# Decode attention with a gated unit: the last pair's values in the slot of the last keys but one, gate's weights in the slot of the values

## The chip, the core and the metric

The kernel runs on one core of one Trainium2 chip. The metric is the device time of one execution in microseconds (us); three executions are given, and one more was profiled. All data are 32-bit floats.

## What is computed

One token passes through an attention over a cache of 8192 keys and values for each of 32 heads, and through a gated linear unit; the product of both is added to the input.

```python
# x: 1 x 512, k_cache and v_cache: 32 heads x 8192 x 128, wq: 512 x 4096, wo: 4096 x 512
xn = layernorm(x)
q = (xn @ wq) by heads                       # 32 x 128
p = softmax((q . k_cache) / sqrt(128))       # 32 x 8192
s = (p @ v_cache, heads side by side) @ wo   # 512
h = sigmoid(xn @ w_gate) * (xn @ w_up)       # 1376
g = silu(h @ w_down)                         # 512
out = x + s * g
```

Keys and values are 134 MB each, the weights some 26 MB. Each byte is read once.

## The kernel before

Heads are taken in 16 pairs (`NP = 16`, i from 0 to 15). A pair's keys, and a pair's values, are one load of 8.4 MB: 128 partitions with 128 rows of 128 elements each, the first head in the lower 64 partitions, the second in the upper 64.

There are three buffers of that size, `slots[0]` to `slots[2]`; together they take most of the core's memory. Keys of pair i go to slot `i % 2` and values of every pair to slot 2 (`issue`, L115 to L117). wq is loaded to slot 2 ahead of everything. The weights of the gated unit (`load_gate`, L88) go to slot `NP % 2`, which is slot 0, in three loads (w_gate and w_up at L92, w_down's first 1280 rows at L95), with a fourth for w_down's last 128 rows into a tile of its own (L96). wo (`load_wo`, L102) goes to slot 1 in five loads (L106).

All of these loads are issued by SP, in the order of the list `order`: wq, keys 0, keys 1, values 0, keys 2, values 1, and so on to keys 15, values 14, values 15, gate, wo. `need(item)` issues the list up to and with that item. An issue waits on SP until the slot's last readers are done, and whatever stands behind it on SP waits too. Each transfer counts up one of eight completion counters that are handed out in turn, and waits for that counter's former transfer.

For pair i the loop does this. VectorE multiplies the keys by the query in place (`times_query`, L263) and sums the rows (`row_sums`, L268), in two halves. Between the first multiplication and the first sum of pair i stand the maximum and the exponentials of pair i - 1 (`all_max`, L278 to L285), the two small DMAs of ScalarE that place the heads of pair i - 2 in `o_all` (`place`, L314), and TensorE's work on the values of pair i - 1 (`values`, L295 to L301). At the end of the loop's body come `need("v", i)`, the next keys, and the row maximum (`row_max`, L272 and L274). So the values of pair i are consumed one turn of the loop after its keys.

Pair 14 (`NP - 2`) has no keys two pairs ahead, and `need` is skipped there; pair 15 issues the rest of the list, up to wo.

After the loop: the values of pair 15, the two matrix products of the gated unit (`glu_row`, L201), `place` of pair 15, the unit's hidden layer and output (`glu_hidden`, L208 to L213; `glu_out`, L228 to L233), and the projection by wo in the five parts in which it lands (`project`, L320 and L324, with a fold over partitions at L219 and L221). VectorE multiplies, adds the input, and SP stores.

Of the kernel before, what the change touches and what calls it, by code (L numbers as in the profile page):

```python
# [18 lines left out]
def kernel(  # L19
# [19 lines left out]
    NP = H // 2  # L39
# [24 lines left out]
    slots = [stream.tile([P, SLOT], F32, name=f"slot{i}") for i in range(3)]  # L64
# [12 lines left out]
    def load_rows(which, src, t, i):  # L77
        rows = src.rearrange("b h s d -> (b h s) d")[2 * i * S:2 * (i + 1) * S, :]
        nc.sync.dma_start(t, rows.rearrange("(p j) d -> p (j d)", p=P))
        kv_t[which, i] = t  # L80
# [5 lines left out]
    assert FW + GP <= QT and FL % GP == 0 and 2 * KT * F + FP * D <= SLOT  # L86

    def load_gate():  # L88
        t = slots[NP % 2]
        for n, (name, src) in enumerate((("wg", w_gate), ("wu", w_up))):  # L90
            v = t[:, n * KT * F:(n + 1) * KT * F].rearrange("p (k f) -> p k f", f=F)
            nc.sync.dma_start(v, src.rearrange("(p k) f -> p k f", k=KT))  # L92
            gl[name] = v
        v = t[:, 2 * KT * F:2 * KT * F + FP * D].rearrange("p (c e) -> p c e", e=D)
        nc.sync.dma_start(v, w_down[:FP * P, :].rearrange("(p r) e -> p r e", r=FP))  # L95
        nc.sync.dma_start(wd_last, w_down[F - P:, :])  # L96
        gl["wd"] = [v[:, c, :] for c in range(FP)] + [wd_last]
# [12 lines left out]
    order = [("wq", 0), ("k", 0)]  # L110
# [3 lines left out]

    def issue(which, i):  # L115
        dict(wq=load_wq, gate=load_gate, wo=load_wo, k=lambda: load_rows("k", k_cache, slots[i % 2], i),
             v=lambda: load_rows("v", v_cache, slots[2], i))[which]()  # L117

    ahead = iter(order)
    loaded = set()  # L120
# [1 line left out]
    def need(*item):  # L122
        while item not in loaded:
            nxt = next(ahead)
            issue(*nxt)
            loaded.add(nxt)
# [54 lines left out]
    def spread(t):  # L181

        b, g = divmod(t, NG)
        pb = big(f"pb{t}")
        nc.tensor.matmul(pb, ones[g * GP:g * GP + 1, :], q_row[g * GP:g * GP + 1, b, :],  # L185
                         start=True, stop=True)
        qb[t] = work.tile([P, 2, Dh], F32, tag="qb", name=f"qb{t}", bufs=2)
        for e, h in enumerate(HALF):
            nc.scalar.copy(qb[t][h], pb.rearrange("p (i e d) -> p i e d", e=2, d=Dh)[h, :, e, :])  # L189
# [71 lines left out]
    def times_query(i, j):  # L261
        q = qb[i // 2][:, i % 2:i % 2 + 1, :]
        nc.vector.tensor_mul(key_rows(i, j), key_rows(i, j), q.to_broadcast([P, SB, Dh]))  # L263

    def row_sums(i, j):
        if j == 0:
            sc[i] = work.tile([P, NB], F32, tag="sc", name=f"sc{i}", bufs=2)
        nc.vector.reduce_sum(sc[i][:, j:j + SB], key_rows(i, j), axis=AX.X)  # L268

    def row_max(i):  # L270
        mx[i] = work.tile([P, 4], F32, tag="mx", name=f"mx{i}", bufs=2)
        nc.vector.reduce_max(mx[i][:, 0:1], sc[i], axis=AX.X)  # L272
        pt = ps_s.tile([1, P], F32, tag="ps_s", name=f"pt{i}")
        nc.tensor.matmul(pt, mx[i][:, 0:1], ident, start=True, stop=True)  # L274
        return pt

    def all_max(i, pt):
        nc.vector.reduce_max(mx[i][:1, 1:3], pt.rearrange("o (e p) -> o e p", e=2), axis=AX.X)  # L278
        pm = ps_s.tile([P, 2], F32, tag="ps_s", name=f"pm{i}")
        nc.tensor.matmul(pm, ones[:1, :], mx[i][:1, 1:3], start=True, stop=True)  # L280
        rs[i] = work.tile([P, 1], F32, tag="rs", name=f"rs{i}", bufs=2)
        for e, h in enumerate(HALF):
            nc.scalar.mul(mx[i][h, 3:4], pm[h, e:e + 1], -SCALE)  # L283
        for e, h in enumerate(HALF):
            nc.scalar.activation(weights[h, :, e * HT:(e + 1) * HT],  # L285
                                 sc[i][h].rearrange("p (g b) -> p g b", b=HT), AF.Exp,
                                 bias=mx[i][h, 3:4], scale=SCALE, accum_out=rs[i][h])

    def values(i):
        row = pn[i % 2]  # L290
        nc.tensor.matmul(row[:, Dh:], half, rs[i], start=True, stop=True)  # L291

        for j in range(0, NB, HT):
            g = j // HT % NG
            nc.tensor.matmul(po[i % 2][g * GP:g * GP + 2 * HT, :], weights[:, j // HT, :],  # L295
                             kv_t["v", i][:, j * Dh:(j + HT) * Dh],
                             start=(j < HT * NG), stop=(j >= NB - HT * NG))
        o1 = work.tile([P, QT], F32, tag="o1", name=f"o1_{i}")
        nc.scalar.copy(o1, po[i % 2])  # L299
        for b in range(HT):  # L300
            nc.tensor.matmul(row[:, :Dh], pick[:, b:2 * HT:HT], o1[:, b * Dh:(b + 1) * Dh],  # L301
                             start=(b == 0), stop=(b == HT - 1))

    def heads_out(i):
        rl = work.tile([2, 1], F32, tag="rl", name=f"rl{i}", bufs=2)
        nc.vector.reciprocal(rl, pn[i % 2][:, Dh:])  # L306
        on = work.tile([2, Dh], F32, tag="on", name=f"on{i}", bufs=2)
        nc.vector.tensor_scalar(on, pn[i % 2][:, :Dh], rl, None, op0=ALU.mult)
        return on

    def place(i, on):
        for e in range(2):
            p0 = (2 * i + e) * WP
            nc.scalar.dma_start(o_all[p0:p0 + WP, :], on[e:e + 1, :].rearrange("o (a r) -> o a r", r=WR))  # L314
# [17 lines left out]
    for i in range(NP):  # L332
        if i % 2 == 1 and i + 1 < NP:
            spread(i // 2 + 1)
        times_query(i, 0)
        if i > 0:
            all_max(i - 1, pt)
            if on is not None:
                place(i - 2, on)
            need("v", i - 1)  # L340
            values(i - 1)
        row_sums(i, 0)
        for j in range(SB, NB, SB):
            times_query(i, j)
            row_sums(i, j)

        need("v", i)
        if i != NP - 2:
            need(*(("k", i + 2) if i + 2 < NP else order[-1]))
        pt = row_max(i)  # L350
        if i > 0:
            on = heads_out(i - 1)
# [42 lines left out]
```

## Time and profile before

| | |
|---|---|
| three runs | 702.3, 703.5, 703.5 us (median 703.5) |
| the profiled execution | 702.62 us |
| its span from first to last instruction | 700.8 us |
| DMA traffic | 294.00 MB, mean 420 GB/s |
| VectorE busy | 576.9 us (82%) |
| TensorE busy (matmuls) | 231.3 us (33%) |
| ScalarE busy | 43.4 us (6%) |
| mean granted TensorE clock | 0.659 of full speed |

The page cuts the span into 40 slices of 17.5 us and prints a busy share for each engine, in tenths, so that a stretch in which something stops is seen at a glance. The chain of work that ended last is followed back from the last instruction, each step to what released it; in order of time it tells what the next step waited for. SPq stands for SP's instruction queue, in which the loads are issued. Times in the rows are in us from the start of the span.

### The profile page before, as it was taken

To read this page: it belongs to the slowest core of one execution; us is meant where nothing else is said; L and a number is where in the kernel's file an instruction comes from. 1 tells how busy PE (TensorE), PEld (TensorE's weight loads), DVE (VectorE), ACT (ScalarE), POOL (GpSimd) and SP (SyncE) were. 2 spreads that over 40 slices of the span, in tenths; PEclk is the share of its full clock that TensorE was granted. 3 is DMA by queue.
4 is the path that set the end of the run, shared out by engine and by line. 5 is a ranking of instruction groups with operands and counts; after the bars stand their busy time and mean duration, and the time that the engine had idled before them with its cause. 6 is when DMAs were issued, how large, how long until landed. Compare 5 with 4: busy or idle time off the path is not lost.

```text
span 700.8 us, 3712 instructions
## 1 busy us (share of the span) xinstructions
PE 231.3 (33%) x1570; PEld 61.7 (9%) x1570; DVE 576.9 (82%) x171; ACT 43.4 (6%) x138; POOL 0.7 (0%) x6
## 2 busy tenths in 40 slices
PE   0510150516051422505061504324061505033556
PEld 0100010101010100101010101001010101001121
DVE  0259999999999989898998989898998989796020
ACT  0010010001010000000001000000001000001010
POOL 0000000000000000000000000000000000000000
PEclk9955575757575575757575666657575756657698
DMA  9999999999999999999999999999999999958996
GB/s 415 423 419 419 464 412 438 420 423 426 460 424 426 427 449 431 430 426 446 430 434 426 442 434 434 431 434 434 438 431 430 434 441 431 430 218 352 391 432 272
DMA packets 6481, 294.00 MB, mean 420 GB/s; under 512 B 1080, under 2 KB 1088, under 8 KB 1472
## 3 DMA queue, kind: packets, MB, share of 16 engines
q1 hardware_dynamic: 6056, 293.74, 97.2%
q8 instruction: 12, 0.20, 0.1%
q10 hardware_dynamic: 408, 0.02, 0.0%
q14 instruction: 5, 0.04, 0.0%
HBM read 293.74 MB, written 0.00 MB: 419 GB/s over the span
## 4 chain that ended last, share of the span: by engine, by line
DMA 68%; PE 19%; DVE 11%; issue 0%; ACT 0%; SPq 0%; ACTq 0%; DVEq 0%
DMA slot<-in_A_v_cache_dram 57%; PE po L295 19%; DVE slot L263 6%; DMA slot<-in_A_k_cache_dram 6%; DMA slot<-in_A_wo_dram 5%; DVE sc L268 5%; PE acc L320 1%; PE acc L324 0%; PE pm L280 0%; ACT s_acc L219 0%; DVE mx L272 0%; ACTq L314 0%; ACT weights L285 0%; SPq L106 0%; DVE mx L278 0%
## 5 line engine op out<-in xcount | busy, mean ns | idle before, releaser
L263 DVE TENSOR_TENSOR slot<-slot,qb 128x8192 f32<-128x8192 f32 x32 | 277.8, 8681 | 43.5 <-DMA slot<-in_A_k_cache_dram 43.5
L268 DVE TENSOR_REDUCE sc<-slot 128x64 f32<-128x8192 f32 x32 | 277.7, 8679 | 0.9 <-DVE mx L278 0.3
L295 PE MATMUL po<-slot,weights 128*8 128x512 f32 x1024 | 147.2, 740 | 104.6 <-DMA slot<-in_A_v_cache_dram 104.6
L280 PE MATMUL pm<-mx,ones 1*128 1x2 f32 x32 | 9.3, 358 | 145.9 <-DVE mx L278 145.9
L274 PE MATMUL pt<-ident,mx 128*1 128x128 f32 x32 | 9.3, 392 | 143.4 <-DVE rl L306 103.2
L295 PEld LDWEIGHTS po<-slot,weights 128*8 128x8 f32 x1024 | 28.7, 104 | 209.8 <-DMA slot<-in_A_v_cache_dram 106.1
L299 ACT COPY o<-po 128x512 f32<-128x512 f32 x16 | 9.4, 585 | 256.6 <-PE po L295 256.6
L280 PEld LDWEIGHTS pm<-mx,ones 1*128 1x128 f32 x32 | 7.9, 306 | 161.3 <-DVE mx L278 161.3
L306 DVE RECIPROCAL rl<-pn 2x1 f32<-2x1 f32 x16 | 2.3, 146 | 23.6 <-PE pn L301 23.6
L301 PE MATMUL pn<-o,pick 128*2 128x128 f32 x128 | 16.6, 272 | 11.5 <-ACT o L299 11.5
L283 ACT ACTIVATE mx<-pm 64x1 f32<-64x1 f32 x32 | 5.3, 165 | 225.5 <-PE pm L280 225.1
L147 DVE TENSOR_REDUCE st<-x_col 128x1 f32<-128x4 f32 x1 | 0.2, 156 | 21.9 <-DMA x_col<-in_A_x_dram 21.9
L185 PE MATMUL pb<-q_row,ones 1*128 1x512 f32 x16 | 15.6, 1075 | 0.0
L274 PEld LDWEIGHTS pt<-ident,mx 128*1 128x1 f32 x32 | 1.8, 80 | 148.1 <-issue 148.1
L285 ACT ACTIVATE weights<-sc,mx 64x128 f32<-64x128 f32 x32 | 12.8, 399 | 0.8
L189 ACT COPY qb<-pb 64x256 f32<-64x256 f32 x16 | 5.9, 366 | 108.1 <-PE pb L185 108.0
L301 PEld LDWEIGHTS pn<-o,pick 128*2 128x2 f32 x128 | 9.6, 84 | 28.6 <-ACT o L299 26.3
L364 DVE TENSOR_TENSOR g_row<-g_row,acc 128x128 f32<-128x128 f32 x1 | 0.3, 289 | 14.2 <-PE acc L324 14.2
L291 PE MATMUL pn<-rs,half 128*2 128x1 f32 x32 | 3.0, 164 | 24.9 <-ACT weights L285 24.9
L320 PE MATMUL acc<-slot,o_all 128*1 128x512 f32 x56 | 9.7, 781 | 3.7 <-DMA slot<-in_A_wo_dram 3.7
L174 PE MATMUL pq<-slot,xn 128*1 128x512 f32 x64 | 9.5, 757 | 1.4 <-DVE pq L165 1.4
L143 PE MATMUL p_sum<-st,ones 128*128 128x1 f32 x2 | 0.6, 362 | 23.3 <-DVE st L147 23.3
(65 smaller groups left out, 65.6 us busy)
## 6 DMA issues: line engine op xcount, KB each, us to landing
slot<-in_A_wo_dram SPq DMA_DIRECT2D x1, 3584.0 KB
slot<-in_B_w_gate_dram SPq DMA_DIRECT2D x1, 2752.0 KB
slot<-in_B_w_up_dram SPq DMA_DIRECT2D x1, 2752.0 KB
slot<-in_B_w_down_dram SPq DMA_DIRECT2D x1, 2560.0 KB
slot<-in_A_wo_dram SPq DMA_DIRECT2D x1, 2560.0 KB
slot<-in_A_wo_dram SPq DMA_DIRECT2D x1, 1024.0 KB
slot<-in_A_wo_dram SPq DMA_DIRECT2D x1, 768.0 KB
o_all<-on ACTq DMA_DIRECT2D x32, 0.5 KB
```

The source lines that it names most:

```text
L174: nc.tensor.matmul(pq[b][g * GP:g * GP + 1, :], xn[:, k:k + 1], gl["wq"][:, k, c:c + QT], start=(k == 0), stop=(k == KT - 1))
L185: nc.tensor.matmul(pb, ones[g * GP:g * GP + 1, :], q_row[g * GP:g * GP + 1, b, :], start=True, stop=True)
L189: nc.scalar.copy(qb[t][h], pb.rearrange("p (i e d) -> p i e d", e=2, d=Dh)[h, :, e, :])
L263: nc.vector.tensor_mul(key_rows(i, j), key_rows(i, j), q.to_broadcast([P, SB, Dh]))
L268: nc.vector.reduce_sum(sc[i][:, j:j + SB], key_rows(i, j), axis=AX.X)
L274: nc.tensor.matmul(pt, mx[i][:, 0:1], ident, start=True, stop=True)
L280: nc.tensor.matmul(pm, ones[:1, :], mx[i][:1, 1:3], start=True, stop=True)
L285: nc.scalar.activation(weights[h, :, e * HT:(e + 1) * HT], sc[i][h].rearrange("p (g b) -> p g b", b=HT), AF.Exp, bias=mx[i][h, 3:4], scale ...
L295: nc.tensor.matmul(po[i % 2][g * GP:g * GP + 2 * HT, :], weights[:, j // HT, :], kv_t["v", i][:, j * Dh:(j + HT) * Dh], start=(j < HT * NG ...
L299: nc.scalar.copy(o1, po[i % 2])
L301: nc.tensor.matmul(row[:, :Dh], pick[:, b:2 * HT:HT], o1[:, b * Dh:(b + 1) * Dh], start=(b == 0), stop=(b == HT - 1))
L320: nc.tensor.matmul(acc4[g:g + 1, :], o_all[:, r:r + 1], gl["wo"][:, r, :], start=(r < NG), stop=(r + NG >= W_FOLD))
```

## The change

Values of pair 15 go to slot `NP % 2`, which is slot 0, in place of slot 2. Gate's weights go to slot 2 in place of slot 0. At the end of pair 14's turn, where nothing was issued beyond its own values, the values of pair 15 are issued as well. The list `order` stays as it is, and so does every instruction of the computing engines.

```diff
     def load_gate():
-        t = slots[NP % 2]
+        t = slots[2]
...
-             v=lambda: load_rows("v", v_cache, slots[2], i))[which]()
+             v=lambda: load_rows("v", v_cache, slots[2 if i < NP - 1 else NP % 2], i))[which]()
...
         need("v", i)
-        if i != NP - 2:
-            need(*(("k", i + 2) if i + 2 < NP else order[-1]))
+        if i + 2 < NP:
+            need("k", i + 2)
+        elif i + 2 == NP:
+            need("v", i + 1)
+        else:
+            need(*order[-1])
         pt = row_max(i)
```

## Rows read from the trace of the kernel before

**Rows 1.** The page: busy time of the engines, GB/s by slice, the chain's shares.

```profile
PE 231.3 (33%) x1570; PEld 61.7 (9%) x1570; DVE 576.9 (82%) x171; ACT 43.4 (6%) x138; POOL 0.7 (0%) x6
...
GB/s 415 423 419 419 464 412 438 420 423 426 460 424 426 427 449 431 430 426 446 430 434 426 442 434 434 431 434 434 438 431 430 434 441 431 430 218 352 391 432 272
...
DMA 68%; PE 19%; DVE 11%; issue 0%; ACT 0%; SPq 0%; ACTq 0%; DVEq 0%
```

**Rows 2.** The chain in order of time, last stage: start, duration, what.

```profile
555.98 29.82 DMA slot<-in_A_v_cache_dram
...
585.84 9.89 PE po L295 x64
...
595.75 29.29 DMA slot<-in_A_v_cache_dram
...
625.08 9.05 PE po L295 x64
...
634.14 21.75 DMA slot<-in_A_v_cache_dram
```

**Rows 3.** The timeline, VectorE and TensorE: start, duration, instruction, idle time before it.

```profile
566.60 8.69 DVE L263 TENSOR_TENSOR slot<-slot,qb 128x8192 f32<-128x8192 f32 x1 [3.14 <-DMA slot<-in_A_k_cache_dram]
...
592.71 8.69 DVE L268 TENSOR_REDUCE sc<-slot 128x64 f32<-128x8192 f32 x1
...
605.78 8.69 DVE L263 TENSOR_TENSOR slot<-slot,qb 128x8192 f32<-128x8192 f32 x1 [3.62 <-DMA slot<-in_A_k_cache_dram]
...
631.90 8.69 DVE L268 TENSOR_REDUCE sc<-slot 128x64 f32<-128x8192 f32 x1
...
644.07 0.19 PE L291 MATMUL pn<-rs,half 128*2 128x1 f32 x2 [1.47 <-ACT weights L285]
...
655.93 8.93 PE L295 MATMUL po<-slot,weights 128*8 128x512 f32 x64 [11.68 <-DMA slot<-in_A_v_cache_dram]
```

**Rows 4.** The timeline of SP's queue: start, duration, load issued.

```profile
562.73 0.33 SPq L79 DMA_DIRECT2D slot<-in_A_k_cache_dram  x1
...
634.56 0.38 SPq L92 DMA_DIRECT2D slot<-in_B_w_gate_dram  x1
...
635.47 0.54 SPq L95 DMA_DIRECT2D slot<-in_B_w_down_dram  x1
```

**Rows 5.** SP's own waits, 600 to 640 and 640 to 701: total, times, longest.

```profile
SPq L79 <- DMA slot<-in_A_v_cache_dram: 29.0, 1, 29.0
SPq L79 <- PE po L295: 9.1, 1, 9.1
...
SPq L96 <- DMA slot<-in_A_v_cache_dram: 19.9, 1, 19.9
...
SPq L106 <- DMA o_all<-on: 4.0, 1, 4.0
```

**Rows 6.** Stretches: length, busy time by engine, clock, DMA share, GB/s.

```profile
625.00:634.20 9.20, 8.99 (x64) 1.74 (x64) 9.16 (x2) 0.05 (x1) 0.00 (x0) 0.78 0.01 2
...
655.90:695.30 39.40, 29.10 (x270) 7.44 (x270) 4.12 (x18) 3.19 (x5) 0.00 (x0) 0.82 0.99 421
...
685.50:688.00 2.50, 2.49 (x12) 0.40 (x16) 0.00 (x0) 0.00 (x0) 0.00 (x0) 0.50 0.97 418
...
690.50:692.00 1.50, 1.24 (x12) 0.19 (x10) 0.00 (x0) 0.00 (x0) 0.00 (x0) 1.00 1.00 415
```

**Rows 7.** The timeline of TensorE after the last pair's values, columns as in rows 3.

```profile
669.11 2.57 PE L201 MATMUL pwu<-slot,xn 128*1 128x320 f32 x56 [0.31 <-DMA slot<-in_B_w_up_dram]
...
676.42 4.01 PE L228 MATMUL pd<-slot,hid 128*1 128x512 f32 x18 [4.74 <-DMA slot<-in_B_w_down_dram]
...
685.51 6.05 PE L320 MATMUL acc<-slot,o_all 128*1 128x512 f32 x28 [3.48 <-DMA slot<-in_A_wo_dram]
...
691.82 3.60 PE L320 MATMUL acc<-slot,o_all 128*1 128x512 f32 x28 [0.26 <-DMA slot<-in_A_wo_dram]
```

## The prediction

> **What bounds the kernel now.** I read the profile's page first. VectorE is busy 82% of the span and TensorE 33%, yet the transfers run at 412 GB/s or more in the first 35 slices, and the chain that ended last is 68% DMA [rows 1]. So the kernel is a stream of 294 MB, and what counts is whether that stream ever stops. Slice 35 (613 to 631 us) falls to 218 GB/s and slice 36 to 352: something stops there and nowhere else before the end [rows 1].
>
> Second I read the chain in order of time over the last stage. It is a plain alternation: a load of values lands, 64 matmuls consume it (9.89 and 9.05 us), the next load of values is issued the moment they end, and so on [rows 2]. In the steady loop that costs nothing: while TensorE consumes values, the engines carry the next keys, already queued. The landings show it: keys of pair 14 at 566.6, values 13 at 585.8, keys 15 at 605.7, values 14 at 625.0, one load of 8.4 MB each 19.2 to 19.9 us [rows 2, 3].
>
> Third, SP's queue, its waits and the stretch itself. After keys 15 there are no more keys to cover the next gap. The load of values 15 targets slot 2, which values 14 hold until the matmuls end at 634.13; it is issued at 634.14 [rows 2]. The queue had waited 29.0 us for values 14 to land and then 9.1 us for their matmuls [rows 5]. From 625.0 to 634.2 the engines moved 2 GB/s [rows 6]. The lone load then takes 21.75 us from issue to landing at 655.89 [rows 2].
>
> Fourth, what follows that landing. Gate's three large loads were issued at 634.6 to 635.5 and lie in the queue behind values 15; the stretch from 655.9 to 695.3 runs at 421 GB/s without a stop [rows 4, 6]. TensorE waits there for w_up 0.31 us, w_down 4.74, the first part of wo 3.48 and the second 0.26 [rows 7]. So the end is paced by the stream.
>
> **The change, part by part.** *Values 15 to slot 0.* Slot 0 held keys 14. VectorE's last pass over them starts at 592.71 and lasts 8.69 us, so the slot is free at 601.4 [rows 3]. SP issues values 14 at 595.75 [rows 2], then stands at this wait for 5.7 us; nothing else is in its queue that could go earlier, since gate needs slot 2 and wo needs slot 1, which VectorE reads until 640.6 [rows 3]. At 601.4 keys 15 are still landing (until 605.7) and values 14 are queued, so values 15 become the third load outstanding. Three outstanding were there at 562.73 too, when keys 15 were issued behind keys 14 (landing 566.6) and values 13, and they landed 19.2 and 19.9 us apart [rows 2, 3, 4]. So values 15 should follow values 14 at that distance: landing at 625.04 + 19.2 to 19.9 = 644.3 to 645.0 instead of 655.89. I take 19.4, the middle of the three distances 19.2, 19.9 and 19.3: 644.4. Gain: 30.85 − 19.4 = 11.4 us (bounds 10.9 and 11.6). The same from the parts: 9.10 us of stopped stream plus 21.75 − 19.4 = 2.35 us for a load that starts on an idle queue.
>
> The Trainium skill, "DMA: Bandwidth & Descriptors", section "Anatomy of one DMA", puts the fixed cost of a transfer at about 2.0 us, there for another issuing path; the gain by it would be 9.1 + 2.0 = 11.1 us. The rows give 2.35, and I go by the rows.
>
> *Gate to slot 2.* The four loads now wait for the matmuls on values 14, at 634.13, in place of values 15. They were issued at 634.56 and after [rows 4], so their issue hardly moves. They must be queued before values 15 finish; a load needs 2.35 us to start, so the last useful moment is 644.4 − 2.35 = 642.0. Cover: 7.4 us. Without it, each us of delay past 642.0 is a us of stopped stream. The smaller fourth load, w_down's last rows, writes no slot and still waited 19.9 us for values 15 to land [rows 5]: some issues also wait for an earlier transfer's completion counter. In the changed kernel it may wait so until 644.4, and wo stands behind it in SP's queue; but w_gate, w_up and w_down (8.3 MB, about 19 us) are queued ahead, so that wait is covered by some 17 us. The last part of wo waited 4.0 us for a small o_all transfer [rows 5]; that transfer comes earlier with the rest.
>
> *The removed condition.* Program order of the other engines is untouched; no instruction is added or taken away, so nothing is to be costed on TensorE, VectorE or ScalarE themselves.
>
> *What is late next.* The weights of pair 15 depend on VectorE: its last pass starts at 631.90 and the first matmul of pair 15 runs at 644.07 [rows 3]. Values 15 would arrive at 644.3 or later, so VectorE's chain and the stream meet within a us; if the weights come last they cost nothing yet, because TensorE next waits for w_up (0.31 us) and w_down (4.74 us), which move with the stream [rows 7]. So everything after the landing moves by 11.4 us with the same distances.
>
> *TensorE's clock in the tail.* The same 64 matmuls took 9.89, 9.05 and 8.93 us [rows 2, 3]; the difference is how soon after an idle stretch the granted clock goes from 0.50 (1.2 GHz) to 1.00 (2.4 GHz), as it does between 688 and 690.5 in the last stage [rows 6]. In the last stage the first part of wo took 6.05 us for 28 matmuls and the second 3.60 for as many, at a wait of only 0.26 us between them [rows 7]. If the rise comes 0.9 us less lucky there, the end moves by 0.9 − 0.26 = 0.6 us. A luckier rise gains nothing, for the second part of wo lands when it lands. Bounds 0 and +0.6; I take +0.2, nearer the two equal rows.
>
> *Sum.* Profiled execution: 702.62 (span 700.8 and 1.8 around it) − 11.4 + 0.2 = 691.4. The four known times, 702.3, 702.62, 703.5 and 703.5, have a mean of 703.0, 0.4 above the profiled one; so 691.8. From the bounds: 702.3 − 11.6 = 690.7 to 703.5 − 10.9 + 0.6 = 693.2.
>
> **The rivals.**
> (a) *Gate is held until values 15 land*, by a reused completion counter as the fourth load was [rows 5]. Then the queue runs dry at 644.4 and restarts 2.35 us later: 694.2. Against it: w_gate went 0.42 us after values 15 [rows 4], so it waited for nothing that was in flight then; and the order of transfers on the counters changes little.
> (b) *The tail stays at the lower clock* because the stages have moved against it: the second part of wo 6.05 instead of 3.60, and the closing 1.9 us of matmuls and fold about double: +4 us, 695.8. Against it: the clock rose within the first part of wo, which ran through [rows 6, 7], and that part keeps its length.
> (c) *Values 14 and 15 share the engines* rather than queue. Values 14 then land late, by up to 19.4 us; their matmuls end late, slot 2 comes free late, and gate with all behind it starts late. The stream stops as soon as values 14 land after 642.0 − 9.05 = 632.9, and the gain is gone when they land at 644.4. There it turns slower: with the matmuls at the slowest pace (the lower clock throughout, about 13.5 us by 6.05 for 28) gate goes out at 657.9, starts at 660.2, against 655.9 before: about +4.4 us, 707. The Trainium skill, same page, section "Queues, rings and completion order", says that an engine takes its descriptors in ring order but that a later one may finish first; the first half speaks against this rival, the second for a trace of it. The rows decide: three loads outstanding landed a full 19.2 and 19.9 us apart [rows 2, 3].
> (d) *The change doesn't do what it says*: a wait for values 14's matmuls remains on values 15, say through the order that the framework keeps. Then 703.5. Against it: keys 15 in slot 1 were issued at 562.73 without regard to values 13 in slot 2 [rows 3, 4], so waits go by slot.
>
> **How the numbers follow.** Forecast 691.8: 0.90. (a) 694.2: 0.04. (b) 695.8: 0.02. (c) 707: 0.02. (d) 703.5: 0.02. The forecast's own range 690.7 to 693.2 and a few tenths for the runs' spread give 690.3 to 693.8, which leaves out (a) to (d) and a little more. A measurement can tell about 0.2% (1.4 us) from no change: faster 0.96, same 0.02, slower 0.02.
>
> **What would show it.** Right: values 15 issued near 601.5 and w_gate near 634.2; more than 400 GB/s in slices 35 and 36; values 15 consumed from 644 to 645, with a wait before them of under 1 us where 11.7 us stood [rows 3]; the waits for w_down and wo as before, all 11 to 12 us earlier; the end of the chain leading from wo back through the stream. Wrong: values 14 landing after 626; a stretch under 300 GB/s around 645; a wait for w_gate; the issue of values 15 near 634.

## The result, and the profile after

The changed kernel takes 690.4 us (median of six runs, 690.0 to 691.8) against 703.3 us: a ratio of 0.982, 95% interval 0.981 to 0.983. That is 12.9 us less; the forecast was 691.8. Between the two profiled executions the span went from 700.8 to 688.7 us, 12.1 us less.

The page of the changed kernel first: transfers in GB/s by slice, and the chain's shares by engine, to be read beside [rows 1].

```profile
GB/s 407 446 426 426 426 412 438 427 426 426 426 432 426 438 457 427 434 426 435 430 426 438 449 431 426 427 445 430 426 439 438 434 426 442 443 426 428 417 423 267
...
DVE 56%; DMA 42%; PE 1%; issue 0%; ACT 0%; ACTq 0%; SPq 0%; DVEq 0%
```

The hole of 218 and 352 GB/s is gone; no slice but the last is below 407. The queue of SP in the same stage (start, duration, load issued; compare [rows 2, 4]):

```profile
601.56 0.33 SPq L79 DMA_DIRECT2D slot<-in_A_v_cache_dram  x1
630.02 0.33 SPq L92 DMA_DIRECT2D slot<-in_B_w_gate_dram  x1
632.84 0.33 SPq L92 DMA_DIRECT2D slot<-in_B_w_up_dram  x1
634.59 0.33 SPq L95 DMA_DIRECT2D slot<-in_B_w_down_dram  x1
645.47 0.33 SPq L96 DMA_DIRECT2D wd_last<-in_B_w_down_dram  x1
```

Values 15 are issued at 601.56 where they went out at 634.14. Gate's loads go out one by one from 630.02, each as soon as the matmuls on its own columns of slot 2 are done. Two stretches (length, busy time of PE, PEld, DVE, ACT, POOL, granted clock, DMA share, GB/s; compare [rows 6]):

```profile
625.00:634.20 9.20, 9.20 (x64) 1.74 (x56) 9.16 (x2) 0.00 (x0) 0.00 (x0) 0.71 1.03 443
...
645.50:683.00 37.50, 29.29 (x270) 7.77 (x270) 4.12 (x18) 3.19 (x5) 0.00 (x0) 0.79 0.98 417
```

While TensorE consumes values 14, the engines now move 443 GB/s instead of 2. TensorE's timeline (start, duration, instruction, idle time before it and what ended it; compare [rows 3, 7]):

```profile
643.63 0.19 PE L291 MATMUL pn<-rs,half 128*2 128x1 f32 x2 [1.48 <-ACT weights L285]
645.50 9.68 PE L295 MATMUL po<-slot,weights 128*8 128x512 f32 x64 [1.68 <-DMA slot<-in_A_v_cache_dram]
...
664.68 3.90 PE L228 MATMUL pd<-slot,hid 128*1 128x512 f32 x18 [2.98 <-DMA slot<-in_B_w_down_dram]
...
673.73 5.77 PE L320 MATMUL acc<-slot,o_all 128*1 128x512 f32 x28 [3.55 <-DMA slot<-in_A_wo_dram]
679.69 3.60 PE L320 MATMUL acc<-slot,o_all 128*1 128x512 f32 x28 [0.19 <-DMA slot<-in_A_wo_dram]
```

The wait for values 15 fell from 11.68 to 1.68 us, and the waits for w_down and wo behind it are still there, some 12 us earlier: the end is paced by the stream as before.

One reading is a trap. The chain that ended last was 68% DMA and is now 56% VectorE, as if the bound had changed. In order of time (start, duration, what) the chain's turn is here:

```profile
642.66 0.41 ACTq L314
...
643.29 6.71 DMA o_all<-on
...
650.01 0.02 SPq L106
...
650.08 29.57 DMA slot<-in_A_wo_dram
...
679.69 3.62 PE acc L320 x28
```

The second part of wo is issued when a small o_all transfer completes (its counter is reused), that transfer comes from ScalarE, and ScalarE waited for VectorE. So the chain runs back through VectorE. But the second part of wo, issued at 650.08, lay behind more than 9 MB already queued (w_up, w_down and the first part of wo), and its first packet started only at 670.0, when they had moved: an issue on the chain is not yet a cause. What decides is whether the transfer engines had work all the time.

**How long they had none.** The page's share of DMA counts a packet where it starts, which blurs short stretches. The trace has each packet's start and length, and each load's completion arrives as 16 increments, one for each engine. (The Trainium skill, "DMA: Bandwidth & Descriptors", section "Why a DMA increments its semaphore by 16 and not by 1", says the same: a transfer runs on up to 16 engines that finish independently, and the semaphore counts them.) The first and last of the 16 increments, in us:

```
                 values 14            values 15
before       622.25 to 625.04     655.47 to 655.89
changed      622.84 to 624.62     642.14 to 645.45
```

A landing is the slowest of 16. In the kernel before, the engines had sent their last packets of values 14 at 621.9 to 624.6 (623.2 on the mean) and sent their first of values 15 at 635.1 to 635.7 (635.35): 12.2 us in which the average engine had nothing. In the changed kernel the time without a packet between 615 and 660 us is 0.09 us per engine. The difference, 12.1 us, is also that of the two spans; that they agree to the tenth is chance, since six runs of the changed kernel differ by up to 1.8 us. I call this time the stop and give it for each experiment, from its one profiled execution.

The stop leaves out one thing. The first 64 KB packet of each engine after it took 2.6 to 3.3 us, where the median of such packets is 2.42: a further 0.7 us per engine. The changed kernel has 0.05 us of this between 620 and 662 us.

### The profile page after: what moved, and what is told of

It reads as the page before. It is cut to its first block, busy times and chain, and to the rows that moved or that the text cites. A ratio compares the mean times of both kernels' runs of the same rounds, so it can differ in the third digit from the quotient of the medians.

```text
span 688.7 us, 3713 instructions
## 1 busy us (share of the span) xinstructions
PE 231.3 (34%) x1570; PEld 62.1 (9%) x1570; DVE 576.9 (84%) x171; ACT 43.4 (6%) x138; POOL 0.7 (0%) x6
## 4 chain that ended last, share of the span: by engine, by line
DVE 56%; DMA 42%; PE 1%; issue 0%; ACT 0%; ACTq 0%; SPq 0%; DVEq 0%
DMA slot<-in_A_k_cache_dram 37%; DVE sc L268 28%; DVE slot L263 28%; DMA slot<-in_A_wo_dram 4%; DMA o_all<-on 1%; PE acc L320 1%; DVE mx L278 0%; DVE mx L272 0%; PE acc L324 0%; DVE on L308 0%; DVE rl L306 0%; PE pt L274 0%; ACT s_acc L219 0%; DVE pwu L165 0%; DVE pwg L165 0%
## 5 line engine op out<-in xcount | busy, mean ns | idle before, releaser
L263 DVE TENSOR_TENSOR slot<-slot,qb 128x8192 f32<-128x8192 f32 x32 | 277.8, 8681 | 43.2 <-DMA slot<-in_A_k_cache_dram 43.2
```

## The experiments

Ratios are against runs of the kernel before that were made beside each experiment; their medians are 702.7 to 702.8 us.

**Which part does it: the slots alone.** The request of values 15 back at its old place, slots as in the change.

```diff
-        if i + 2 < NP:
-            need("k", i + 2)
-        elif i + 2 == NP:
-            need("v", i + 1)
-        else:
-            need(*order[-1])
+        if i != NP - 2:
+            need(*(("k", i + 2) if i + 2 < NP else order[-1]))
```

> Only the slots change: values 15 to slot 0, gate to slot 2, with the request at its old place, the end of pair 15's turn. SP issues in the order of the list, and nothing stands between values 14 and values 15 there. My theory: the whole gain, 690.4 us, values 15 issued near 601.5. Rival (the place of the request counts): 703.3, or at least later than 690.4 by some us because the issue waits for something of pair 15's turn.

Measured 689.8 us (0.981, interval 0.978 to 0.983), stop 0.08 us. SP's queue:

```profile
601.15 0.33 SPq L79 DMA_DIRECT2D slot<-in_A_v_cache_dram  x1
629.81 0.33 SPq L92 DMA_DIRECT2D slot<-in_B_w_gate_dram  x1
```

The whole gain comes with the slots. The third hunk of the diff moves a request that SP reaches at the same moment either way, so the rival of the earlier request falls.

**The request alone.** The counterpart, with both slots as before.

```diff
-        if i != NP - 2:
-            need(*(("k", i + 2) if i + 2 < NP else order[-1]))
+        if i + 2 < NP:
+            need("k", i + 2)
+        elif i + 2 == NP:
+            need("v", i + 1)
+        else:
+            need(*order[-1])
```

> Only the place of the request moves: values 15 are asked for at the end of pair 14's turn, but still into slot 2, and gate still goes to slot 0. My theory (the time goes with the stretch in which the transfer engines stand still, and that goes with the slot): nothing changes, 703.3 us, values 15 issued near 634.1 after 29 and 9 us of waits. Rival (asking earlier is what counts): near 690.4. A mixed rival would lie between.

Measured 700.0 us, which neither side expected. I had overlooked that the request now stands ahead of the matmuls on values 14 in the program while both use slot 2: the load no longer waits for these matmuls, they wait for it, and pair 14 is computed from values 15. Timeline of TensorE (columns as above):

```profile
646.27 8.97 PE L295 MATMUL po<-slot,weights 128*8 128x512 f32 x64 [29.93 <-DMA slot<-in_A_v_cache_dram]
...
659.70 8.74 PE L295 MATMUL po<-slot,weights 128*8 128x512 f32 x62
```

The stop is only 2.5 us, but two blocks of matmuls and everything behind them now follow the late landing one after another, and TensorE sets the end. So this run doesn't answer its question, which the one before did. It shows that a request may move ahead in the program only together with its slot.

**Values 15 in slot 0, gate left in slot 0, its request where it was.**

```diff
-        t = slots[2]
+        t = slots[NP % 2]
```

> Values 15 go to slot 0 as in the changed kernel, but gate stays in slot 0 too, so its loads wait for the matmuls on values 15. My theory: the stop is not gone but comes one load later. Values 15 land near 645.5; w_gate's columns are free after about 5.4 us of matmuls (630.02 less 624.67 in the changed kernel), so it is issued near 650.9 and starts 1.3 us later, while the engines ran out of values 15 at 643.6 on the mean (16 landings from 642.1 to 645.5): 8.6 us of stop, 690.4 + 8.6 = 699.0. Rival (the early load of values 15 is the gain, gate's slot is only its consequence): 690.4. Rival (all of the gain is lost without both): 703.3.

Measured 699.7 us, near the 699.0, but not for the reason given. Gate's request stands ahead of the matmuls on values 15, so it overwrites them as soon as they have landed; pair 15 is computed from gate's weights. Timeline of TensorE:

```profile
653.26 5.30 PE L295 MATMUL po<-slot,weights 128*8 128x512 f32 x20 [9.92 <-DMA slot<-in_B_w_gate_dram]
659.77 2.75 PE L295 MATMUL po<-slot,weights 128*8 128x512 f32 x22 [1.22 <-DMA slot<-in_B_w_up_dram]
665.84 4.39 PE L295 MATMUL po<-slot,weights 128*8 128x512 f32 x22 [3.32 <-DMA slot<-in_B_w_down_dram]
```

The matmuls wait for w_gate, w_up and w_down. The agreement of the time is chance, and I repeated the question in a form that keeps the order of the work.

**The same half, with gate's request behind the matmuls on values 15.**

```diff
-        t = slots[2]
+        t = slots[NP % 2]
...
         elif i + 2 == NP:
             need("v", i + 1)
-        else:
-            need(*order[-1])
...
     values(NP - 1)
+    need(*order[-1])
     glu_row("wg")
```

> One half of the change alone, in a form that computes everything: values 15 go to slot 0 and are asked for at the end of pair 14's turn, but gate stays in slot 0, and its request (and wo's behind it) stands after the matmuls on values 15 in the program. My theory: the stop is moved behind values 15 and shortened, not removed. Values 15 land near 645.5, w_gate's columns are free after some 5.4 us of matmuls, so w_gate goes out near 650.9 and its first packets 1.3 us later, at 652.2, while the engines run out of values 15 at 643.6 on the mean: 8.6 us of stop, 690.4 + 8.6 = 699.0. Rival (gate's slot is a mere consequence, the early values are the gain): 690.4. Rival (nothing is left of the gain with one half): 703.

Measured 699.1 us (0.995, 0.993 to 0.996); stop 8.88 us between 641.7 and 652.3. SP's queue:

```profile
650.28 0.33 SPq L92 DMA_DIRECT2D slot<-in_B_w_gate_dram  x1
653.07 0.33 SPq L92 DMA_DIRECT2D slot<-in_B_w_up_dram  x1
```

and two stretches (columns as above):

```profile
645.50:652.00 6.50, 6.50 (x41) 1.25 (x37) 0.00 (x0) 0.00 (x0) 0.00 (x0) 0.61 0.21 47
652.00:690.00 38.00, 24.61 (x218) 6.43 (x214) 4.12 (x18) 3.19 (x5) 0.00 (x0) 0.78 0.99 419
```

Here the stop stands behind values 15 in place of values 14, and it is 3.3 us shorter, because gate's columns come free piece by piece. (The 643.6 of the expectation is a little late: in the changed kernel the engines' last packets of values 15 ended at 643.0 on the mean, in this run at 642.8; the first packets came 0.6 us earlier than expected too, at 651.6, so the length of the stop came out near.) So gate's move to slot 2 is worth 8.7 us, and the early values alone some 3.6. Both rivals fall.

**The stop by doses.** In the next three, slot 0 is held longer: VectorE copies one column of keys 14 after a later step of pair 15, and values 15 are issued behind it. The edit to the changed kernel, in its first form (of the three calls the one acts whose two numbers agree; the others have 2 and 3 for the first number):

```diff
+    held = const.tile([P, 1], F32, name="held")
+
+    def hold(i, at, here):
+        if i == NP - 1 and at == here:
+            nc.vector.tensor_copy(held, kv_t["k", NP - 2][:, 0:1])
+            need("v", NP - 1)
...
         row_sums(i, 0)
+        hold(i, 1, 1)
         for j in range(SB, NB, SB):
             times_query(i, j)
+            hold(i, 1, 2)
             row_sums(i, j)
+            hold(i, 1, 3)
...
-        if i + 2 < NP:
-            need("k", i + 2)
-        elif i + 2 == NP:
-            need("v", i + 1)
-        else:
-            need(*order[-1])
+        if i != NP - 2:
+            need(*(("k", i + 2) if i + 2 < NP else order[-1]))
```

So nothing is asked for at the end of pair 14's turn, as in the kernel before.

> The changed kernel with slot 0 held longer: VectorE copies one column of keys 14 (some 0.1 us) after its sums over the first half of keys 15, near 622.9, and values 15 are issued only then instead of at 601.5. My theory: nothing is lost until the 16 engines run out of values 14 (623.0 on the mean, landings 622.8 to 624.6) less the 1.3 us that a load needs to its first packet, so to 621.7; from there each us costs one. Here 1.2 us: 691.6. Rival (an early issue is worth something by itself, 21 us earlier or later): between 691.6 and 703.3 in proportion, about 698.

> The same, with the copy after the multiplication of the second half of keys 15, near 631.6. My theory: 631.6 - 621.7 = 9.9 us of stop, 700.3. Rival (the gain of the change came mainly from the tail, where everything stands otherwise, and not from the stop): near 691.

> The same, with the copy after the last sums over keys 15, near 640.3, later than the kernel before issued values 15 (634.14). My theory: 640.3 - 621.7 = 18.6 us of stop, 709.0, slower than the kernel before by 5.7. Rival (beyond the stop of the kernel before something else covers, since the weights of pair 15 are ready only at 643.6): about 703.

Measured 693.2, 701.3 and 710.3 us (ratios 0.987, 0.998 and 1.011), with values 15 issued at 623.82, 632.57 and 641.48 and stops of 0.84, 9.51 and 17.93 us. SP's issues of values 15 in the first and the third:

```profile
623.82 0.33 SPq L79 DMA_DIRECT2D slot<-in_A_v_cache_dram  x1
...
641.48 0.33 SPq L79 DMA_DIRECT2D slot<-in_A_v_cache_dram  x1
```

SP's longest wait in the second (total, times, longest):

```profile
SPq L79 <- DVE held L334: 35.5, 1, 35.5
```

and its queue:

```profile
632.57 0.33 SPq L79 DMA_DIRECT2D slot<-in_A_v_cache_dram  x1
633.00 0.37 SPq L92 DMA_DIRECT2D slot<-in_B_w_gate_dram  x1
```

An issue 22 us later than in the changed kernel cost 2.8 us, with a stop of 0.84, since values 14 still covered nearly all of it; the next two cost a further 8.1 and 9.0 us for stops longer by 8.7 and 8.4. The last is slower than the kernel before, as its stop is longer. All three came out 1.0 to 1.6 us above the numbers expected. Their values 14 landed at 625.6 to 625.9, 1.0 to 1.3 us later than in the changed kernel, so this was there before the held slot mattered. Most of it shows in the packets: up to 600 us a 64 KB packet took 2.426 to 2.428 us on the mean in these three, against 2.423 in the changed kernel (medians of 2.421 and 2.418, the latter in all the other kernels too), which over the 226 that an engine moves by then is 0.7 to 1.0 us. What makes these packets slower, and where the rest comes from, is open. One number in the expectations is off as well: in the changed kernel the last packets of values 14 ended at 623.6 on the mean (622.5 to 624.3), not 623.0. With 623.6 the stops expected are 0.6, 9.3 and 18.0 us, close to the 0.84, 9.51 and 17.93 measured, and the times lie 1.6 to 2.2 us above what follows.

**The stop cut without moving a slot.** The kernel before, with values 15 in four loads by columns.

```diff
-        nc.sync.dma_start(t, rows.rearrange("(p j) d -> p (j d)", p=P))
+        rows = rows.rearrange("(p j) d -> p (j d)", p=P)
+        parts = 4 if (which, i) == ("v", NP - 1) else 1
+        for c in range(0, SLOT, SLOT // parts):
+            nc.sync.dma_start(t[:, c:c + SLOT // parts], rows[:, c:c + SLOT // parts])
```

> The kernel before with its slots, but values 15 loaded in four DMAs by columns (2.1 MB each), so that the first can go out when a quarter of the matmuls on values 14 is done. My theory: the first quarter is issued about 3.5 us after values 14 land, near 628.6 instead of 634.14; the stop shrinks by 5.6 us, and the following quarters are free before the engines need them (a quarter takes 4.8 us to move, its matmuls at most 3.4): 703.3 - 5.6 = 697.7. Rival (the restart of a lone load, and not the wait, is the price): four smaller loads restart just as the one did, 703.3 or later. Values 15 would land near 650.3.

Measured 696.8 us (0.991, 0.988 to 0.994); stop 6.54 us. SP's queue (four issues merged):

```profile
628.07 5.86 SPq L82 DMA_DIRECT2D slot<-in_A_v_cache_dram  x4
```

and two stretches:

```profile
625.00:628.00 3.00, 3.00 (x20) 0.63 (x16) 3.00 (x1) 0.00 (x0) 0.00 (x0) 0.50 0.00 0
628.00:634.00 6.00, 5.52 (x49) 1.00 (x40) 5.96 (x2) 0.40 (x1) 0.00 (x0) 0.95 0.87 322
```

The first quarter went out at 628.07 and the stop is 5.7 us shorter, as worked out; the last quarter landed at 651.3, the expectation had 650.3. Nearly half of the gain is to be had with no other slot. The rival, that restarting is the price, falls: the restart is there, with slow first packets that cost 0.7 us per engine, and yet the kernel is faster.

**Another cover: gate ahead of the last values.** Slots as before; the list's end and the gated unit moved.

```diff
-    order += [("v", NP - 1), ("gate", 0), ("wo", 0)]
+    order += [("gate", 0), ("v", NP - 1), ("wo", 0)]
...
-        if i != NP - 2:
-            need(*(("k", i + 2) if i + 2 < NP else order[-1]))
+        need(*(("k", i + 2) if i + 2 < NP else ("gate", 0) if i + 2 == NP else order[-1]))
...
-    values(NP - 1)
     glu_row("wg")
     glu_row("wu")
-    place(NP - 1, heads_out(NP - 1))
     glu_out(glu_hidden())
+    values(NP - 1)
+    place(NP - 1, heads_out(NP - 1))
```

> Another cover for the same stop: slots as in the kernel before, but gate is loaded to slot 0 ahead of values 15 (slot 0 is free at 601.4), and values 15 follow in slot 2 once the matmuls on values 14 are done, near 634.1, while gate is still moving; the gated unit is computed ahead of the last values. My theory: the stream does not stop, but its end is no longer the end: values 15 land near 665, their matmuls take 9 to 10 us, the heads' small transfers some 6, and all 56 matmuls on wo come after that: span near 697, time 698 (694 to 701). Rival (a stream without a stop is enough, whatever its order): 690.4.

Measured 698.7 us (0.995, 0.993 to 0.997), with a stop of 0.15 us. The chain at its end:

```profile
633.63 30.61 DMA slot<-in_A_v_cache_dram
...
664.28 9.68 PE po L295 x64
...
676.31 4.63 DMA o_all<-on
...
681.62 8.69 PE acc L320 x56
```

The stream doesn't stop here either, and yet the kernel is 8 us slower than the changed one: the last values land at 664.2, and their matmuls, the heads' small transfers (4.6 us) and all of wo's matmuls follow in a row while the engines run out of work. Both have to hold: no stop, and little work behind the last landing.

**All together.** Stop per engine (615 to 660 us, in the one profiled execution), median time, and their difference. The two runs that compute something else are left out, and so is the order with gate first, whose end isn't set by the stream.

```
                       stop    time     time - stop
changed                0.09    690.4      690.3
slots alone            0.08    689.8      689.7
held, first half       0.84    693.2      692.4
split, old slots       6.54    696.8      690.3
gate behind            8.88    699.1      690.2
held, second product   9.51    701.3      691.8
before                12.20    703.3      691.1
held, last sums       17.93    710.3      692.4
```

Over 18 us of stop the difference stays within 2.7 us, so a us of stop costs a us. The three held kernels carry the 1 to 2 us named above. For the kernel before, its runs beside the experiments (702.7 us) give 690.5 in the last column.

In the packets each stop, of 0.84 us as of 17.93, has the slow first packets behind it, 0.7 to 0.8 us per engine in all six kernels with a stop, and 0.05 or less in the two without. So a restart loses some 0.7 us of the stream besides the stop's length. The times, medians of four to ten runs, are too coarse to show it: split and gate behind lie level with the changed kernel.

## Why the prediction was right, point by point

**The bound and the mechanism** held: a stream that stops once, for want of a free slot. Values 15 out at 601.56 (forecast 601.4 to 601.5), values 14 and 15 in order without sharing the engines, no stop left, the tail moved as a whole. Rival (d) fell with the issue at 601.56, rival (c) with values 14 landing at 624.6, rival (a) with w_gate at 630.02, rival (b) with the second part of wo at 3.60 us.

**The term that was mis-sized** is the gain of the stop: 11.4 us with bounds of 10.9 and 11.6, while 12.1 were there. I took it as a difference of landings, 30.85 less 19.4. But a landing is the slowest of 16 engines. The last before the stop, values 14, came at the end of a running stream, with 2.8 us between the first engine and the last; the one after it had all engines start within 0.6 us and finish within 0.4 us, so it hid part of what had been lost. In the changed kernel values 15 come at the end of a running stream again and land 20.8 us after values 14, at 645.45, outside my 644.3 to 645.0: by landings the gain would be 10.4 us. The rest shows behind it: from that landing to the end of the span are 43.2 us instead of 44.9, because engines that were through with values 15 were already moving gate. The measured price of the stop lies in the engines' packets: 12.2 us without one, and the 0.7 us by which the first ones after it are slow.

The Trainium skill, "DMA: Bandwidth & Descriptors", section "Anatomy of one DMA", has a fixed cost of about 2.0 us, for another issuing path; the estimate from it and the 9.1 us of empty stretch was 11.1 us. By parts the rows gave 9.10 + 2.35 = 11.45. That sum was nearer, but not its parts. The average engine ran dry at 623.2, 1.9 us ahead of the landing at 625.04, so the stretch without a packet up to the issue at 634.14 was 11.0 us and not 9.1. The restart took 1.2 us on the mean from the issue to the first packets and 0.7 us in slow ones, 1.9 together, less than 2.35. What both sums leave out is the spread with which the engines ran dry.

**The clock in the tail**, +0.2 us (0 to +0.6), was 0: the first part of wo took 5.77 us against 6.05, and the second part's wait stayed at 0.19 us.

**Gate's issue** was forecast at 634.2, with a cover until 642.0; it came at 630.02 to 634.59 because each load waits for its own columns only. It made no difference under that cover, as the stop of 0.09 us shows. With w_gate at 650.28, behind the matmuls on values 15, the cover was overrun, and the stop was 8.88 us; where the limit lies, no run measured.

**What is late next** was drawn nearly right: TensorE began pair 15 at 643.63 and then waited 1.68 us for values 15 (forecast under 1). The fourth load of gate waited for values 15 until 645.47, and wo behind it, covered as worked out.

**The sum** of 691.4 for the profiled execution met 690.5, and 691.8 for the median met 690.4; of these, 0.7 us are the stop's size and 0.2 the clock. The rest is within what runs of one kernel differ. My range reached down to 690.3 and held the result by a tenth of a us. That was luck: the bounds as worked out, 690.7 to 693.2, miss 690.4, and only the few tenths added for the spread of the runs took it in. The lower end came from bounds on landings, and these bounded the wrong thing.

**Of the signs named**, four did not come: values 15 were consumed from 645.50 and not from 644 to 645, the wait before them was 1.68 us and not under 1, w_gate went out at 630.02 and not near 634.2, and the chain's end leads from wo back through a small transfer to VectorE and not through the stream. The first two are the landing again, the third is the free columns, and the fourth is the trap described above. One sum was off without weight: 6.05 us for 28 matmuls make 13.8 us for 64, not 13.5, which moves rival (c) by 0.3 us.

## What to carry to other kernels

In a kernel bound by one stream of loads, look for the slice where the stream stops, and count the stop on the engines' packets, not from landing to landing; here a us of it was a us of the time. At the end of a rotation of buffers the buffer that would have taken the next load of another kind is free: give it to the load that would otherwise wait, and check that the loads behind it still find their place before the queue runs dry. Cover alone is not enough: of two orders without a stop, the one with less work behind the last landing was 8 us faster here.

## What the runs showed of the hardware that I had not expected

The 16 engines drift apart in a running stream: the increments of one load of 8.4 MB came within 0.4 us after a common start in the kernel before, and within 1.7 to 3.3 us in the flow (loads issued after 200 us, before and changed). A load asked for on an idle queue had its first packets 1.0 to 1.6 us after the issue (634.14 to 635.1 and 635.7), and these took 2.6 to 3.3 us in place of 2.42. A 0.5 KB transfer of the heads beside a running stream took 4.5 to 14 us from issue to landing (the two on the chains shown 4.6 and 6.7 us), in nine traces, where the 64 matmuls on a pair's values take 8.4 to 10; the two that were issued in "gate behind" as its engines ran dry, at 642.5 and 643.1, took 1.6. Whatever waits for one must not stand on the path.
